# Two ScalarE copies moved up between a unit's products, and the last unit's sums and store rearranged

## The chip, the core and the metric

The kernel runs on one core of a Trainium2 chip. The metric is the device time of one execution in microseconds. The engines are TensorE (PE, with its weight loads as PEld), VectorE (DVE), ScalarE (ACT), GpSimd (POOL) and SyncE (SP), which only issues DMAs here.

## The reference

```python
a = softmax(phi, axis=2)                  # batch, n_heads, seq, n_mem = 8, 8, 576, 32
k_m, v_m = einsum('bhsm,bhsd->bhmd', a, k), einsum('bhsm,bhsd->bhmd', a, v)
attn = softmax(q @ k_m.T / sqrt(64))      # head_dim 64
x = (attn @ v_m) as (4608, 512)
h = x @ w_in                              # 512 x 2048
out = (h - tanh(h)) @ w_out               # 2048 x 512, f32
```

Tokens are pooled into 32 memory slots per head, attended to from every token, and put through a two-layer network whose middle function is h - tanh(h).

## The kernel before

Operands in f32 are split into a high and a low f16 part, and each product of TensorE is a sum of products of parts. The 4608 tokens are taken in 18 units of 256 (`UT`), and the 2048 middle columns in four blocks of 512 (`fb`), so there are 72 steps (u, fb). The attention of the eight batches, the conversion of the weights and checks of their range are spread over the steps by tables (`START`, `PLAN`, `PLAN3`, `PLAN_C`). The engines take their instructions in the order of the program text (`in_order`).

From unit 4 on, a step does the following. `mm1` computes the block's middle values into the PSUM tile `hs`. Then a chain of ScalarE and VectorE turns them into g = h - tanh(h) by a short polynomial: ScalarE squares `hs` into `u` (L579), VectorE multiplies (`g1`, L587), ScalarE squares again (`g1_square`, L592), VectorE multiplies (`g2`, L597), ScalarE rounds to f16 (`g2_high`, L603), and POOL forms the low part (`g3`, L608). VectorE also forms sums and differences of blocks of g, the tile `f` (`a_forms`, L621).

The second layer, `mm2_blocks`, runs two steps behind `mm1` and takes seven block products in place of eight (Winograd's form of Strassen's method on 2 x 2 blocks). m1, m5, m6 and m7 accumulate in the PSUM tile `x`, shape 128 x 2 x 512 f32: m1 in `x[:, 0, lo]`, m5 in `x[:, 0, hi]`, m6 in `x[:, 1, lo]`, m7 in `x[:, 1, hi]`, where `lo` and `hi` are the first and second 256 columns. m2, m3 and m4 go straight into the output accumulators `o[0]` and `o[1]`, as does `main`, the one product that the low parts don't double. Each of m1 to m7 is four matmuls (`prod`, L715), `main` is L708, and L702 in the last unit, where a part of `o[1]` goes to a PSUM tile of its own, `oh`. There is one tile `x` for the whole run.

After the fourth block of a unit (`last`) the four parts of `x` are combined. ScalarE copies m1 into `ra[:, 1]` (L753) and m5 into `rb[:, 2]` (L754), where `ra` and `rb` are SBUF tiles (`r` in the profile). Later in the step `evict` has VectorE add m6 and m7 to them (L768, L769), form two more sums (L770, L773), add `o[0]` and `o[1]` (L780, and L777 in the last unit) and store 128 rows at a time (L781 on SP; the last 128 rows at L778 on ScalarE's queue).

In the text of a step, `mm1` and the square at L579 come first, then L587, L592, `a_forms`, L597, then `mm2_blocks` with the two copies, then L603 and the rest. So the copies stand behind L592 on ScalarE. Waits between engines are worked out by the framework from the order of the text, tile by tile: an instruction that writes a tile waits for those ahead of it in the text that read it, and one that reads it waits for those ahead that wrote it.

Of the kernel before, what the change touches and what calls it, by code (L numbers as in the profile page):

```python
# [14 lines left out]
ALU = mybir.AluOpType  # L15
# [3 lines left out]
P = 128  # L19
# [4 lines left out]
NUNIT = B * S // UT  # L24
# [313 lines left out]
def split_path(ctx, tc, c, ins, out):  # L338
    nc = tc.nc
# [295 lines left out]
    acc = {}  # L635
# [50 lines left out]
    def mm2_blocks(u, fb, first, last):  # L686

        f, gg = gs.pop((u, fb))
        x = acc["x"]
        if first:
            acc[u] = [ps_o.tile([P, DM], F32, tag=f"o{i}", name=f"o{u}{fb}{i}") for i in range(2)]
        o = acc[u]
        ws = (wout_hi, wout_lo)

        def main(th):
            if th and u == NUNIT - 1:
                for dst, cs, end in ((acc["h1"], hi, last), (o[1][:, lo], lo, False)):  # L700
                    for k in range(4):
                        nc.tensor.matmul(  # L702
                            dst, gg[:, 0, k, P : 2 * P], wout_hi[:, 4 * fb + k, cs],
                            start=(first and k == 0), stop=(end and k == 3),
                        )
                return
            for k in range(4):
                nc.tensor.matmul(  # L708
                    o[th], gg[:, 0, k, P * th : P * th + P], wout_hi[:, 4 * fb + k, :], start=(first and k == 0), stop=False
                )  # L710

        def prod(dst, a, b, new=False, end=False):
            for kk in range(2):
                for n in range(2):
                    nc.tensor.matmul(  # L715
                        dst, a(1 - n, kk), b(n, kk), start=(new and kk == 0 and n == 0), stop=(end and kk == 1 and n == 1)
                    )

        def ab(th, kh):
            return lambda n, kk: gg[:, n, 2 * kh + kk, P * th : P * th + P]  # L720

        def af(i):
            return lambda n, kk: f[:, n, i, kk]

        def bb(kh, nh):
            return lambda n, kk: ws[n][:, 4 * fb + 2 * kh + kk, 256 * nh : 256 * nh + 256]

        def bf(i):
            return lambda n, kk: bts[i][:, n, fb, kk]

        lo, hi = slice(0, 256), slice(256, 512)
        if first and u == NUNIT - 1:
            acc["h1"] = ps_a.tile([P, 2, 512], F32, tag="pa", name="oh")[:, 0, lo]
        m1 = (x[:, 0, lo], ab(0, 0), bb(0, 0), first)
        m2 = (o[0][:, lo], ab(0, 1), bb(1, 0))
        m3 = (o[0][:, hi], af(0), bb(1, 1))
        m4 = (o[1][:, lo], ab(1, 1), bf(3))
        m5 = (x[:, 0, hi], af(2), bf(0))
        m6 = (x[:, 1, lo], af(3), bf(1), first)
        m7 = (x[:, 1, hi], af(1), bf(2))  # L740
        if not last:
            for m in (m1, m5, m6, m7) if first else ():
                prod(*m)
            main(0)
            main(1)
            for m in (m2, m4, m3) if first else (m2, m4, m1, m5, m6, m7, m3):
                prod(*m)
            return
        sc = 1.0 / (S_G * S_W)
        ra, rb = (big.tile([P, 3, 256], F32, tag="pr", name=f"r{u}{i}") for i in range(2))  # L750
        for m, end in ((m1, False), (m5, True), (m6, False), (m7, True)):
            prod(*m, end=end)
        nc.scalar.activation(ra[:, 1], x[:, 0, lo], AF.Copy, scale=sc)  # L753
        nc.scalar.activation(rb[:, 2], x[:, 0, hi], AF.Copy, scale=sc)  # L754
        for th, ms in ((0, (m2, m3)), (1, (m4,))):
            main(th)
            for m in ms:
                prod(*m, end=m is ms[-1])
        acc["evict"] = (u, ra, rb)

    def evict():
        if "evict" not in acc:
            return
        u, ra, rb = acc.pop("evict")
        x, o, t0 = acc["x"], acc[u], u * UT
        sc = 1.0 / (S_G * S_W)
        lo, hi = slice(0, 256), slice(256, 512)
        nc.vector.scalar_tensor_tensor(ra[:, 0], x[:, 1, lo], sc, ra[:, 1], op0=ALU.mult, op1=ALU.add)  # L768
        nc.vector.scalar_tensor_tensor(rb[:, 0], x[:, 1, hi], sc, ra[:, 0], op0=ALU.mult, op1=ALU.add)  # L769
        nc.vector.tensor_tensor(ra[:, 2], ra[:, 0], rb[:, 2], op=ALU.add)  # L770
        for th, r in ((0, ra[:, 1:3]), (1, rb[:, 0:2])):
            if th == (u == NUNIT - 1):
                nc.vector.tensor_tensor(rb[:, 1], rb[:, 0], rb[:, 2], op=ALU.add)  # L773
            r = r.rearrange("p a x -> p (a x)")
            if u == NUNIT - 1 and th == 1:
                for cs, p in ((hi, acc["h1"]), (lo, o[1][:, lo])):
                    nc.vector.scalar_tensor_tensor(r[:, cs], p, sc, r[:, cs], op0=ALU.mult, op1=ALU.add)  # L777
                nc.scalar.dma_start(out[t0 + P :, :], r)  # L778
                continue
            nc.vector.scalar_tensor_tensor(r, o[th], sc, r, op0=ALU.mult, op1=ALU.add)  # L780
            nc.sync.dma_start(out[t0 + P * th : t0 + P * th + P, :], r)  # L781
# [114 lines left out]
    for sl, (u, fb) in enumerate(slots, 18):  # L896
# [20 lines left out]
        queue.append((u, fb))  # L917
        v, vb = queue.pop(0)
        mm2_blocks(v, vb, vb == 0, vb == NFB - 1)
        while squared:  # L920
            window_sum(*squared.pop(0))
# [3 lines left out]
        while due and due[0][0] == "C":  # L925
            step(due.pop(0), True)
        evict()
        forms.append((u, fb))
        do(2)
# [3 lines left out]
    for u, fb in queue:  # L933
        mm2_blocks(u, fb, fb == 0, fb == NFB - 1)
    c["wide"] = nc.values_load(c["bad"][0:1, 0:1], min_val=0, max_val=1)
    evict()
    in_order(tc, c["first"])

# [215 lines left out]
```

## Time and profile before

| | |
|---|---|
| median of 3 runs | 659.96 us (659.03 to 661.41) |
| profiled execution, its own time | 659.43 us |
| its span, first to last instruction | 657.6 us |
| granted TensorE clock, mean | 0.995 |
| busy PE / DVE / ACT / POOL | 642.2 / 523.6 / 375.8 / 251.0 us |
| copies L753 and L754, 14 of each | 5.1 and 5.2 us busy |
| products into `x` (L715) | 896 matmuls |
| stores of `r`, 28, 256 KB each | 2.4 us from issue to landing (median) |

Times in rows are in microseconds from the span's start. "Idle before" and an arrow name the instruction that ended an engine's idle time. Matmuls overlap: a row's duration is from its start to its modelled end, while the next one starts earlier. The granted clock is the share of full speed that TensorE was given. The profiled execution's time is 1.83 us over its span, and 0.53 under the median.

### The profile page before, as it was taken

How to read it: one execution, taken by the hardware profiler on the slowest of the kernel's cores; microseconds unless marked ns; L12 is line 12 of the kernel's file. 1: busy time of each engine (PE TensorE's matmuls, PEld its weight loads, DVE VectorE, ACT ScalarE, POOL GpSimd, SP SyncE). 2: the span in 40 equal slices, each digit the busy share in tenths (PEclk: the TensorE clock that was granted, in tenths of full speed). 3: DMA queues.
4: the chain of work that ended last, by engine and by line, in shares of the span. 5: the costliest groups of instructions: out<-in, count | busy, mean ns of one | idle time of the engine just before them, and what ended most of it. 6: DMA issues, size and time to landing. Idle time of an engine off the chain costs nothing.

```text
span 657.6 us, 15599 instructions
## 1 busy us (share of the span) xinstructions
PE 642.2 (98%) x6690; PEld 456.3 (69%) x6690; DVE 523.6 (80%) x790; ACT 375.8 (57%) x509; POOL 251.0 (38%) x173
## 2 busy tenths in 40 slices
PE   8889999999999999999999999999999999999996
PEld 4355656566557777777776677877687777887885
DVE  6899999999855787875898679777978686867773
ACT  4577686666424456545655466545654677666541
POOL 0225141222222245451535353624452555455531
PEclk9899999999999999999999999999999999999999
DMA  9999345301423301324331515142415333234201
GB/s 343 377 365 393 109 170 180 117 3 65 146 97 102 138 28 74 113 91 145 105 113 66 168 51 168 37 162 70 146 41 197 98 101 117 63 117 136 86 33 37
DMA packets 25996, 84.98 MB, mean 129 GB/s; under 512 B 2880, under 2 KB 2880, under 8 KB 25152
## 3 DMA queue, kind: packets, MB, share of 16 engines
q1 hardware_dynamic: 24624, 81.55, 35.9%
q10 hardware_dynamic: 1296, 2.36, 0.9%
q8 instruction: 54, 0.88, 0.6%
q14 instruction: 22, 0.18, 0.1%
HBM read 72.37 MB, written 11.53 MB: 128 GB/s over the span
## 4 chain that ended last, share of the span: by engine, by line
PE 79%; DVE 11%; DMA 4%; ACT 2%; issue 2%; POOL 1%; SPq 0%; DVEq 0%; ACTq 0%; POOLq 0%
PE hs L572 20%; PE x L715 13%; PE o L708 13%; PE o L715 10%; PE o L651 6%; PE h L572 4%; PE o1h L651 3%; PE pp L524 3%; DMA raw<-in_w_out_dram 2%; PE pkv L220 2%; DMA kv<-in_kva_dram 2%; PE warm L789 1%; DVE wt L384 1%; DVE h L597 1%; DVE h L587 1%
## 5 line engine op out<-in xcount | busy, mean ns | idle before, releaser
L608 POOL TENSOR_TENSOR g<-h,g 128x1024 f16<-128x1024 f32 x64 | 138.5, 2165 | 327.3 <-ACT g L603 233.3
L572 PEld LDWEIGHTS <-ph 128*128 128x128 f16 x2304 | 176.9, 98 | 20.5 <-issue 6.0
L572 PE MATMUL hs<-ah,ph 128*128 128x256 f16 (+3 forms) x1152 | 151.5, 246 | 0.0
L587 DVE SCALAR_TENSOR_TENSOR h<-hs,u 128x1024 f32<-128x1024 f32 x54 | 65.8, 1219 | 91.0 <-ACT u L579 90.9
L603 ACT ACTIVATE g<-h 128x1024 f16<-128x1024 f32 x72 | 75.9, 1055 | 92.3 <-DVE h L597 90.2
L572 PE MATMUL hs<-al,ph 128*128 128x256 f16 (+3 forms) x576 | 127.6, 246 | 0.0
L592 ACT ACTIVATE u<-u,beta 128x1024 f32<-128x1024 f32 x72 | 82.4, 1147 | 55.5 <-DVE h L587 54.4
L708 PE MATMUL o<-wout_hi,g 128*128 128x512 f16 x432 | 104.7, 379 | 0.0
L715 PEld LDWEIGHTS <-f 128*128 128x128 f16 x896 | 87.7, 98 | 10.1
L597 DVE SCALAR_TENSOR_TENSOR h<-u,h 128x1024 f32<-128x1024 f32 x72 | 87.4, 1216 | 0.8 <-ACT u L592 0.7
L579 ACT ACTIVATE u<-hs 128x1024 f32<-128x1024 f32 x54 | 55.0, 1019 | 52.8 <-PE hs L572 48.3
L715 PEld LDWEIGHTS <-g 128*128 128x128 f16 x672 | 64.2, 98 | 26.5 <-issue 5.1
L715 PE MATMUL x<-bt,f 128*128 128x256 f16 x672 | 82.5, 273 | 0.0
L708 PEld LDWEIGHTS <-g 128*128 128x128 f16 x432 | 40.5, 98 | 43.9 <-issue 8.1
L621 DVE TENSOR_TENSOR f<-g 128x512 f16<-128x512 f16 x112 | 65.7, 626 | 4.3 <-POOL g L608 3.4
L651 PEld LDWEIGHTS <-g 128*128 128x128 f16 x384 | 36.7, 98 | 46.5 <-issue 3.4
L651 PE MATMUL o<-wout_hi,g 128*128 128x512 f16 x192 | 58.8, 379 | 0.0
L572 PE MATMUL h<-ah,ph 128*128 128x256 f16 (+3 forms) x384 | 49.6, 246 | 0.1
L572 PE MATMUL h<-al,ph 128*128 128x256 f16 (+2 forms) x192 | 42.4, 246 | 0.2 <-POOL al L515 0.2
L542 DVE SCALAR_TENSOR_TENSOR ph<-pp,ph 128x1024 f16<-128x1024 f32 x31 | 37.6, 1213 | 0.6 <-ACT ph L537 0.6
L537 ACT ACTIVATE ph<-pp 128x1024 f16<-128x1024 f32 x32 | 32.5, 1017 | 7.5 <-PE pp L524 7.4
L651 PE MATMUL o<-wout_lo,g 128*128 128x512 f16 x96 | 36.4, 379 | 0.0
(146 smaller groups left out, 980.0 us busy)
## 6 DMA issues: line engine op xcount, KB each, us to landing
kv<-in_kva_dram SPq DMA_DIRECT2D x20, 516.0 KB, 4.1
q<-in_qt_dram SPq DMA_DIRECT2D x16, 576.0 KB, 4.9
chk<-in_w_in_dram SPq DMA_DIRECT2D x16, 512.0 KB, 5.7
chk<-in_w_out_dram SPq DMA_DIRECT2D x16, 512.0 KB, 3.4
out_dram<-r SPq DMA_DIRECT2D x27, 256.0 KB, 2.4
kv<-in_kva_dram SPq DMA_DIRECT2D x6, 1032.0 KB, 8.8
raws<-in_w_in_dram SPq DMA_DIRECT2D x12, 512.0 KB, 7.1
raw<-in_w_out_dram SPq DMA_DIRECT2D x12, 512.0 KB, 7.2
```

Source lines behind the costliest of these rows:

```text
L542: nc.vector.scalar_tensor_tensor(pl, pa, S_P / (S_V * S_W), ph, op0=ALU.mult, op1=ALU.subtract)
L572: nc.tensor.matmul(hp[:, k, tu : tu + w], px[:, g, cs], d[ax][:, g, ta : ta + w], start=(n == 0), stop=(n == 5),)
L579: nc.scalar.activation(uu, hp, AF.Square, scale=1.0 / (S_A * S_P))
L587: nc.vector.scalar_tensor_tensor(h3, hp, C2 * S_G / (S_A * S_P), uu, op0=ALU.mult, op1=ALU.mult)
L592: nc.scalar.activation(uu, uu, AF.Square, bias=c["beta"])
L597: nc.vector.scalar_tensor_tensor(h3, uu, CC, hp, op0=ALU.add, op1=ALU.mult)
L603: nc.scalar.activation(gg[:, 0], h3, AF.Copy)
L608: eng.tensor_tensor(gg[:, 1], h3, gg[:, 0], op=ALU.subtract)
L621: nc.vector.tensor_tensor(o, x, y, op=op)
L651: nc.tensor.matmul(o, gx[:, k, P * tt : P * tt + P], wx[:, 4 * fb + k, :], start=(first and k == 0 and wx is wout_hi and gx is gh), stop=( ...
L708: nc.tensor.matmul(o[th], gg[:, 0, k, P * th : P * th + P], wout_hi[:, 4 * fb + k, :], start=(first and k == 0), stop=False)
L715: nc.tensor.matmul(dst, a(1 - n, kk), b(n, kk), start=(new and kk == 0 and n == 0), stop=(end and kk == 1 and n == 1))
```

## The change

In a unit's last block the two copies are issued behind m1 and m5 and ahead of m6 and m7. In `evict` the add L773 always stands ahead of the sums with `o`; in the last unit it stood between them. The last unit's second 128 rows are stored in two halves of 256 columns, each as soon as its sum is there, the first on SP and the second on ScalarE's queue.

```diff
-        for m, end in ((m1, False), (m5, True), (m6, False), (m7, True)):
+        for m, end in ((m1, False), (m5, True)):
             prod(*m, end=end)
         nc.scalar.activation(ra[:, 1], x[:, 0, lo], AF.Copy, scale=sc)
         nc.scalar.activation(rb[:, 2], x[:, 0, hi], AF.Copy, scale=sc)
+        for m, end in ((m6, False), (m7, True)):
+            prod(*m, end=end)
...
         nc.vector.tensor_tensor(ra[:, 2], ra[:, 0], rb[:, 2], op=ALU.add)
+        nc.vector.tensor_tensor(rb[:, 1], rb[:, 0], rb[:, 2], op=ALU.add)
         for th, r in ((0, ra[:, 1:3]), (1, rb[:, 0:2])):
-            if th == (u == NUNIT - 1):
-                nc.vector.tensor_tensor(rb[:, 1], rb[:, 0], rb[:, 2], op=ALU.add)
             r = r.rearrange("p a x -> p (a x)")
             if u == NUNIT - 1 and th == 1:
-                for cs, p in ((hi, acc["h1"]), (lo, o[1][:, lo])):
+                for cs, p, q in ((hi, acc["h1"], nc.sync), (lo, o[1][:, lo], nc.scalar)):
                     nc.vector.scalar_tensor_tensor(r[:, cs], p, sc, r[:, cs], op0=ALU.mult, op1=ALU.add)
-                nc.scalar.dma_start(out[t0 + P :, :], r)
+                    q.dma_start(out[t0 + P :, cs], r[:, cs])
                 continue
```

No engine's order changes in units 4 to 16; what changes is who waits. On TensorE, unit 4's last block, from m5's last product (`bt0`, weights from `f43`) to m6 (`bt1`); the names in brackets are the semaphores of the engines waited for:

```order
 L715 MATMUL x_2448<-bt0_1865,f43_2746 128x256
 L715 LDWEIGHTS f43_2746 [waits DVE_49]
-L715 MATMUL x_2448<-bt1_2110,f43_2746 128x256
+L715 MATMUL x_2448<-bt1_2110,f43_2746 128x256 [waits Activation_49]
 L715 LDWEIGHTS f43_2746
 L715 MATMUL x_2448<-bt1_2110,f43_2746 128x256
```

m6's first product has a wait for ScalarE that it had not; the count that it waits for is that of the second copy, L754. All fourteen units have it. A step later on TensorE, at m1 of unit 5 (`g50`), the first product that overwrites `x`:

```order
 L524 LDWEIGHTS vh3_2741
 L524 MATMUL pp30_2931<-win_lo_98,vh3_2741 32x512
-L715 LDWEIGHTS g50_2792 [waits DVE_49,Pool_49]
-L715 MATMUL x_2448<-wout_hi_99,g50_2792 128x256 [waits Activation_49]
+L715 LDWEIGHTS g50_2792 [waits Pool_49]
+L715 MATMUL x_2448<-wout_hi_99,g50_2792 128x256 [waits DVE_49]
 L715 LDWEIGHTS g50_2792
 L715 MATMUL x_2448<-wout_lo_100,g50_2792 128x256
```

The wait for the same count of ScalarE stood here, a step behind the copies, and is gone from here. On VectorE, the sums of the last unit (`r170` is `ra`, `r171` is `rb`, `o1700` and `o1701` are `o[0]` and `o[1]`), before:

```order
L768 SCALAR_TENSOR_TENSOR r170_8660<-x_2448,r170_8660 128x256 [waits DMAHW0_49,PE_49,Activation_49]
L769 SCALAR_TENSOR_TENSOR r171_8661<-x_2448,r170_8660 128x256 [waits DMAHW1_49,DVE_49]
L770 TENSOR_TENSOR r170_8660<-r170_8660,r171_8661 128x256
L780 SCALAR_TENSOR_TENSOR r170_8660<-o1700_8491,r170_8660 128x512 [waits DVE_49,PE_49]
L773 TENSOR_TENSOR r171_8661<-r171_8661 128x256
L777 SCALAR_TENSOR_TENSOR r171_8661<-oh_8493,r171_8661 128x256 [waits DVE_49,PE_49]
L777 SCALAR_TENSOR_TENSOR r171_8661<-o1701_8492,r171_8661 128x256 [waits PE_49]
```

and with the change:

```order
L770 SCALAR_TENSOR_TENSOR r170_8660<-x_2448,r170_8660 128x256 [waits DMAHW0_49,PE_49,Activation_49]
L771 SCALAR_TENSOR_TENSOR r171_8661<-x_2448,r170_8660 128x256 [waits DMAHW1_49,DVE_49]
L772 TENSOR_TENSOR r170_8660<-r170_8660,r171_8661 128x256
L773 TENSOR_TENSOR r171_8661<-r171_8661 128x256 [waits DVE_49]
L781 SCALAR_TENSOR_TENSOR r170_8660<-o1700_8491,r170_8660 128x512 [waits DVE_49,PE_49]
L778 SCALAR_TENSOR_TENSOR r171_8661<-oh_8493,r171_8661 128x256 [waits DVE_49,PE_49]
L778 SCALAR_TENSOR_TENSOR r171_8661<-o1701_8492,r171_8661 128x256 [waits PE_49]
```

The add L773 has moved ahead of the sum with `o[0]`; the two sums of the second half stand where they stood, and a store follows each.

## The prediction

> **What bounds the kernel now.** I read the page first, then the busy time of one long middle stretch, then the waits of TensorE.
>
> ```profile
> span 657.6 us, 15599 instructions
> PE 642.2 (98%) x6690; PEld 456.3 (69%) x6690; DVE 523.6 (80%) x790; ACT 375.8 (57%) x509; POOL 251.0 (38%) x173
> ```
>
> From 60 to 650 us (view by stretches; after the stretch and its length: PE, PEld, DVE, ACT and POOL busy, then the granted clock, DMA share and GB/s):
>
> ```profile
> 60.00:650.00 590.00, 588.31 (x6145) 425.96 (x6144) 470.43 (x696) 339.50 (x450) 238.01 (x155) 1.00 0.32 106
> ...
> PE pkv L220 <- DMA kv<-in_kva_dram: 1.3, 2, 1.0
> ```
>
> TensorE stands still for 1.69 of those 590 us. All that is added to TensorE's stream is added to the time, and at most 1.7 us of idle time can be taken back by a later wait that shrinks. So the question at every edit is what TensorE must wait for.
>
> **Where the moved copies stand.** The timeline of unit 4's last step, all engines; columns are start, duration, engine, line, operation:
>
> ```profile
> 222.09 1.02 ACT L579 ACTIVATE u<-hs 128x1024 f32<-128x1024 f32 x1 [2.56 <-PE hs L572]
> 222.32 1.47 PE L715 MATMUL x<-bt,f 128*128 128x256 f16 x12
> 223.14 1.22 DVE L587 SCALAR_TENSOR_TENSOR h<-hs,u 128x1024 f32<-128x1024 f32 x1 [2.93 <-ACT u L579]
> ...
> 224.40 1.15 ACT L592 ACTIVATE u<-u,beta 128x1024 f32<-128x1024 f32 x1 [1.29 <-DVE h L587]
> ...
> 225.46 0.37 ACT L753 ACTIVATE r<-x 128x256 f32<-128x256 f32 x1
> 225.72 0.37 ACT L754 ACTIVATE r<-x 128x256 f32<-128x256 f32 x1
> ...
> 226.23 0.60 PE L715 MATMUL o<-bt,g 128*128 128x256 f16 x4
> ...
> 228.34 1.28 DVE L780 SCALAR_TENSOR_TENSOR r<-o,r 128x512 f32<-128x512 f32 x2
> ...
> 229.55 1.02 ACT L579 ACTIVATE u<-hs 128x1024 f32<-128x1024 f32 x1 [1.43 <-PE hs L572]
> ```
>
> The row of twelve products holds m5 (four), m6 and m7. They start every (1.47 - 0.27) / 11 = 0.109 us, so m6 starts at 222.32 + 4 x 0.109 = 222.76. ScalarE gets to the copies only at 225.46, because they are queued behind a chain that begins when mm1 ends: square of hs, VectorE's L587, square L592, copies. They do not wait for the products at all; over the whole run they did once, in the last unit:
>
> ```profile
> its engine sat idle before it (us, times) until:
>   PE x L715: 5.2, 1
> ```
>
> So letting the copies wait for eight products in place of sixteen starts no copy earlier in units 4 to 16: the gain there is nil. But the order shows that m6's first product now waits for ScalarE; in the text it comes behind the copies, and it writes the tile x that they read. Before, this wait stood on the next unit's m1, where the copies were long done. The second copy ends at 226.09, 3.33 us after m6 started. Behind m6 on TensorE's queue stand m7, main and m2 to m4, then the next mm1, so TensorE stands still.
>
> **The stalls.** The same stretch, from m6's start to the second copy's end, for units 4 to 16 (columns as above; shortest, one of the middle, longest and the sum):
>
> ```profile
> 222.76:226.09 3.33, 3.33 (x26) 2.33 (x24) 2.91 (x6) 2.04 (x4) 0.00 (x0) 1.00 0.99 375
> ...
> 288.05:290.50 2.45, 2.45 (x21) 1.82 (x19) 2.28 (x6) 1.69 (x3) 0.83 (x1) 1.00 0.80 258
> ...
> 355.46:358.16 2.70, 2.70 (x23) 2.04 (x21) 2.57 (x3) 1.69 (x3) 2.18 (x2) 1.00 0.85 266
> ...
> 459.66:463.23 3.57, 3.57 (x27) 2.44 (x25) 3.44 (x5) 2.34 (x6) 3.48 (x4) 1.00 0.42 119
> ...
> 529.01:533.12 4.11, 4.11 (x38) 2.93 (x36) 2.95 (x3) 2.82 (x6) 3.97 (x4) 1.00 0.34 107
> 562.66:567.14 4.48, 4.48 (x48) 3.29 (x46) 2.92 (x5) 3.19 (x6) 3.16 (x3) 1.00 0.29 99
> ...
> sum 42.70, PE 42.70 PEld 30.42 DVE 37.25 ACT 27.65 POOL 32.09; mean PE 3.28 PEld 2.34 DVE 2.87 ACT 2.13 POOL 2.47
> ```
>
> Seven stalls lie at 3.33 to 3.57, four at 2.45 to 2.70, two above 4. TensorE is busy for all 42.70 us now and would be idle in them. The chain hangs on mm1's end, not on m6, so the stall does not shorten itself. I add 0.03 per unit from the end of a copy to the start of who waits, as in the last unit below: 13 x 0.03 = 0.4. **Stalls: 43.1 us.**
>
> VectorE is also queued behind this: its sum with o[1] (second of the two at 228.34) must wait for m4, which ends at 226.23 + 0.60 = 226.83 now and about 230.2 then. That work is done near 230.9, while the next square, now at 229.55, moves to 232.9: VectorE is free before its next L587. TensorE gets no second wait from it.
>
> **The clock.** A stall of 3 us may also slow the matmuls after it. The granted clock in this run falls twice, at 26.71 and at 654.76, 184 lengths of 3.413 us apart, so I cut the run on that grid (columns as above):
>
> ```profile
> 19.88:23.29 3.41, 2.25 (x52) 1.12 (x50) 2.72 (x7) 2.27 (x4) 1.23 (x2) 1.00 1.02 367
> 23.29:26.71 3.42, 1.58 (x26) 0.77 (x26) 2.99 (x6) 1.94 (x7) 1.04 (x1) 1.00 1.00 376
> 26.71:30.12 3.41, 3.41 (x37) 0.65 (x22) 3.07 (x5) 1.23 (x2) 0.88 (x1) 0.50 0.93 355
> ...
> 651.35:654.76 3.41, 0.98 (x10) 0.64 (x7) 1.77 (x4) 0.00 (x0) 0.00 (x0) 1.00 0.41 153
> 654.76:657.57 2.81, 0.00 (x0) 0.00 (x0) 0.00 (x0) 0.00 (x0) 0.00 (x0) 0.50 0.10 31
> ```
>
> A window in which TensorE was busy for 2.25 us kept the clock; after one with 1.58, and one with 0.98, the next ran at 0.50. What half costs, by warm-up products of one shape inside and behind the slow window:
>
> ```profile
> 27.18 1.03 PE L789 MATMUL warm<-nid 128*128 128x512 f16 x2
> ...
> 30.12 1.03 PE L789 MATMUL warm<-nid 128*128 128x512 f16 x4
> ```
>
> Two products take what four take after it: a slow window loses half of the 3.41 us, 1.71, less half of the idle time that reaches into it.
>
> A stall of s leaves s - 0.16 idle, since m5's last product ends 0.16 behind the next one's slot. Where the window border cuts it is chance. With the limit at 3.42 - 1.58 = 1.84 us idle and a stall of 3.35 (idle 3.19): the first part is over 1.84 in 40% of the positions (loses 1.37 on average, as 0.68 of the idle time reaches into the slow window); the second part in another 40%, or all lies in one window in 6% (1.71 each); in 14% both parts are short and nothing is lost: 1.33 on average. The short ones give 1.0, the long ones 1.55, the sum 7 x 1.35 + 4 x 1.0 + 2 x 1.55 = 16.6. With the limit at 3.41 - 2.25 = 1.16 idle, the same working gives 1.85, 1.64 and 1.97: 23.4. I take 20, between the two. If dense products count for more than the small ones of the start did, only the row at 651.35 is a safe limit (2.43 idle): 0.84, 0 and 1.14, so 9.
>
> The Trainium skill, "TensorE: Matmul & The Clock Gate", section "What's actually happening", has the clock halved after at least one wholly idle window of about 3.4 us; by that the clock term would be near 0.6. The rows at 23.29 and 651.35 speak against it, each halved after a window with work in it.
>
> **The last unit.** Here nothing else holds ScalarE:
>
> ```profile
> 647.82 1.47 PE L715 MATMUL x<-bt,f 128*128 128x256 f16 x12
> 649.33 0.38 ACT L753 ACTIVATE r<-x 128x256 f32<-128x256 f32 x1 [5.24 <-PE x L715]
> 649.61 0.38 ACT L754 ACTIVATE r<-x 128x256 f32<-128x256 f32 x1
> 650.02 0.42 DVE L768 SCALAR_TENSOR_TENSOR r<-x,r 128x256 f32<-128x256 f32 x1 [2.14 <-ACT r L754]
> ...
> 651.74 0.60 PE L715 MATMUL o<-bt,g 128*128 128x256 f16 x4
> ...
> 652.81 0.41 DVE L777 SCALAR_TENSOR_TENSOR r<-o,r 128x256 f32<-128x256 f32 x1
> 653.25 0.38 ACTq L778 DMA_DIRECT2D out_dram<-r  x1
> ...
> DMA to landing us min/median/max: 2.4/2.4/2.4
> ```
>
> m5 ends at 648.42, so the copies run from 648.46 to 649.12 (0.66 both) and m6 starts at 649.15 in place of 648.26: TensorE 0.89 later, its last product ends at 653.23. The last VectorE sum then starts at 653.26 in place of 652.81 and the store at 653.70: 0.45 later. VectorE's own chain moves only by m7's end, 650.02 to 650.23, and has room; the add that now stands ahead of the first half's sum (0.42) lies in the wait for o[0]. The other half of the store goes to SP behind one earlier store, off the path. The last transfer has half the bytes; a 256 KB store lands in 2.4 us, and half of one is not in the trace: between 0 and 0.5 less, I take 0.2, as most of a small store is latency. **End: +0.25** (-0.05 to +0.45).
>
> **Sum**, on the profiled execution (659.43 us, span 657.6, 0.5 under the median of the runs): 659.43 + 43.1 + 20 + 0.3 = 722.8 us.
>
> **Rivals.**
> - Only a nearly idle window slows the clock, as at 651.35: 659.43 + 43.1 + 9 + 0.3 = 712. For it: small-array products filled the window at 23.29, and they may count less. Against: so they did in the one at 19.88, which kept the clock.
> - Stalls without a slower clock, by the skill's whole window: in this mechanism only the stalls of 3.57, 4.11 and 4.48 can hold one: 703.4.
> - Not slower: m6's wait is met early. It would need the copies done by m6's start, over 2.45 us sooner than they are in every unit; that decides. Then the end gains: VectorE's first sum starts at m7's end, 649.3, and the last at 652.4 behind m4, 0.4 early, with 0.2 from the store: 658.8, no measurable change. The Trainium skill, "PSUM — Partial Sum Buffer", section "PSUM bank collisions raise a hardware error", asks for guards by bank and quadrant, not by address. Copies and m6 touch different halves of x, 512 f32 each, one bank each by that page; a wait by bank would leave m6 free, but the order shows the wait.
> - The slow clock lasts two windows per stall: 20 more, 743. Against: the clock was back after one at 30.12.
>
> **Chances.** The likeliest, slowed by nearly every stall: 0.65 (719 to 727). Slowed by some: 0.17 (708 to 716). Whole windows only: 0.10. Not slower: 0.03. Two windows: 0.05. From 708 to 728 leaves out 0.18. Two executions agree within some 2 us, 0.3%, which is what a measurement can tell here; all cases but one are slower by more: slower 0.97, same 0.02, faster 0.01.
>
> **What would show it.** On TensorE thirteen gaps of 2.3 to 4.4 us ahead of m6, put down to ACT's r at L754; copies that still start behind the square of u; the granted clock at 0.50 in ten to sixteen windows, each behind such a gap; TensorE idle some 43 us more in the middle stretch. Wrong would be: no such gaps, or gaps with the clock at full, or a VectorE or POOL wait that turns up on TensorE in the steps between.

## The result and the profile after

The changed kernel takes 720.26 us (median of 6 runs, 718.24 to 722.13) against 659.96: a ratio of 1.0912, interval 1.0888 to 1.0935, 60 us slower. The forecast was 722.8, range 708 to 728. The profiled execution took 718.24 us, with a span of 716.5. Its page, then the stretch from 60 us to shortly before the last unit's copies, then TensorE's waits (columns as ahead):

```profile
span 716.5 us, 15592 instructions
...
PE 660.4 (92%) x6690; PEld 462.5 (65%) x6690; DVE 530.0 (74%) x790; ACT 376.0 (52%) x509; POOL 250.4 (35%) x173
```

```profile
60.00:704.00 644.00, 604.10 (x6119) 429.56 (x6118) 476.44 (x694) 339.30 (x448) 237.44 (x155) 0.97 0.29 97
```

```profile
PE x L715 <- ACT r L754: 37.3, 13, 4.0
PE x L715 <- DVE f L621: 3.3, 1, 3.3
```

TensorE stands still for 39.9 us of that stretch, where before it was 1.7, and all but 0.1 of it lies ahead of m6. The two rows together are fourteen gaps, one a unit; one of them (3.3) is put down to a VectorE row that ended about then. The last unit's gap is 0.75, so the thirteen others are 37.3 + 3.3 - 0.75 = 39.85 us. Unit 4, the same rows as before the change:

```profile
222.33 1.02 ACT L579 ACTIVATE u<-hs 128x1024 f32<-128x1024 f32 x1 [2.56 <-PE hs L572]
...
222.56 0.60 PE L715 MATMUL x<-bt,f 128*128 128x256 f16 x4
223.38 1.22 DVE L587 SCALAR_TENSOR_TENSOR h<-hs,u 128x1024 f32<-128x1024 f32 x1 [2.93 <-ACT u L579]
...
224.64 1.15 ACT L592 ACTIVATE u<-u,beta 128x1024 f32<-128x1024 f32 x1 [1.29 <-DVE h L587]
...
225.70 0.37 ACT L753 ACTIVATE r<-x 128x256 f32<-128x256 f32 x1
225.96 0.38 ACT L754 ACTIVATE r<-x 128x256 f32<-128x256 f32 x1
...
226.39 1.86 PE L715 MATMUL x<-bt,f 128*128 128x256 f16 x8 [3.22 <-ACT r L754]
```

The row of twelve products has split into four (m5) and eight (m6, m7). The copies start where they did beside the chain (directly behind L592), and m6 starts 0.05 us behind the second. The eight then take 1.86 us in place of 1.03. The windows of the clock show why:

```profile
222.33:225.74 3.41, 0.83 (x8) 0.59 (x7) 2.32 (x5) 2.12 (x3) 0.00 (x0) 1.00 0.98 365
225.74:229.15 3.41, 2.76 (x11) 1.57 (x11) 2.24 (x5) 1.65 (x4) 0.72 (x1) 0.50 0.38 153
229.15:232.57 3.42, 3.42 (x27) 2.51 (x26) 3.36 (x6) 0.00 (x0) 1.41 (x1) 1.00 0.00 0
259.87:263.28 3.41, 1.13 (x16) 0.88 (x14) 2.00 (x2) 1.76 (x2) 3.41 (x3) 1.00 0.00 0
263.28:266.70 3.42, 2.41 (x10) 1.43 (x10) 2.96 (x6) 3.04 (x7) 0.03 (x1) 0.50 0.03 5
266.70:270.11 3.41, 3.41 (x13) 1.76 (x12) 3.41 (x4) 0.25 (x1) 2.36 (x1) 0.50 0.00 0
372.51:375.92 3.41, 1.52 (x28) 1.06 (x21) 2.42 (x3) 2.12 (x3) 3.25 (x2) 1.00 0.49 138
375.92:379.34 3.42, 2.95 (x22) 2.15 (x22) 3.35 (x8) 1.36 (x3) 0.00 (x0) 1.00 0.45 176
```

After 0.83 us of work the next window ran at half clock; after 1.52 it kept its speed. Ten of the thirteen stalls slowed the clock, two of them for two windows (263.28 is the first). In the twelve slow windows TensorE was busy for 37.2 us; taken as half of that, the loss is 18.6 us.

### The profile page after: what moved, and what is told of

Same layout as the page of the kernel before. It is cut to its first block, busy times and chain, and to the rows that moved or that the text cites. A ratio compares the mean times of both kernels' runs of the same rounds, so it can differ in the third digit from the quotient of the medians.

```text
span 716.5 us, 15592 instructions
## 1 busy us (share of the span) xinstructions
PE 660.4 (92%) x6690; PEld 462.5 (65%) x6690; DVE 530.0 (74%) x790; ACT 376.0 (52%) x509; POOL 250.4 (35%) x173
## 4 chain that ended last, share of the span: by engine, by line
PE 68%; DVE 18%; ACT 7%; issue 4%; DMA 3%; POOL 0%; SPq 0%; ACTq 0%; DVEq 0%; POOLq 0%
PE hs L572 16%; PE o L708 12%; PE x L715 11%; PE o L715 9%; PE o L651 5%; DVE h L587 5%; PE h L572 4%; ACT u L579 3%; DVE f L621 3%; PE o1h L651 3%; PE pp L524 2%; DVE h L597 2%; DMA raw<-in_w_out_dram 2%; PE warm L790 1%; DVE wt L384 1%
## 5 line engine op out<-in xcount | busy, mean ns | idle before, releaser
L715 PE MATMUL x<-bt,f 128*128 128x256 f16 x672 | 90.6, 284 | 40.6 <-ACT r L754 37.3
L715 PEld LDWEIGHTS <-f 128*128 128x128 f16 x896 | 90.7, 101 | 56.2 <-issue 43.0
L708 PE MATMUL o<-wout_hi,g 128*128 128x512 f16 x432 | 113.4, 403 | 0.0
L592 ACT ACTIVATE u<-u,beta 128x1024 f32<-128x1024 f32 x72 | 82.4, 1147 | 50.9 <-DVE h L587 49.8
L715 PEld LDWEIGHTS <-g 128*128 128x128 f16 x672 | 65.6, 100 | 29.7 <-issue 9.4
L708 PEld LDWEIGHTS <-g 128*128 128x128 f16 x432 | 42.9, 103 | 48.8 <-issue 14.5
L651 PEld LDWEIGHTS <-g 128*128 128x128 f16 x384 | 36.7, 98 | 46.5 <-issue 3.4
L621 DVE TENSOR_TENSOR f<-g 128x512 f16<-128x512 f16 x112 | 60.6, 581 | 3.8 <-POOL g L608 3.4
L651 PE MATMUL o<-wout_hi,g 128*128 128x512 f16 x192 | 58.8, 379 | 0.0
```

The costliest lines, as they stand in the source:

```text
L592: nc.scalar.activation(uu, uu, AF.Square, bias=c["beta"])
L621: nc.vector.tensor_tensor(o, x, y, op=op)
L651: nc.tensor.matmul(o, gx[:, k, P * tt : P * tt + P], wx[:, 4 * fb + k, :], start=(first and k == 0 and wx is wout_hi and gx is gh), stop=( ...
L708: nc.tensor.matmul(o[th], gg[:, 0, k, P * th : P * th + P], wout_hi[:, 4 * fb + k, :], start=(first and k == 0), stop=False)
L715: nc.tensor.matmul(dst, a(1 - n, kk), b(n, kk), start=(new and kk == 0 and n == 0), stop=(end and kk == 1 and n == 1))
```

## The experiments

Beside each is the median of before on the same chip in the same rounds (660.22 for the first four, 660.04 for the last four). The theory: m6 waits for the second copy only because m6 and the copies share the tile x; the copies end late because of their place on ScalarE; and the gaps halve the clock. The rival causes: the sums and stores of the last unit, a cost of the wait as such, and a slower clock that has nothing to do with the gaps.

### The copies alone

The first hunk of the change and nothing else.

> Only the copies are moved; sums and store as before. If m6's wait for the second copy is the cause: thirteen gaps of 2.1 to 4.0 us on TensorE ahead of m6, ten to thirteen half-clock windows, 717.5 to 721 us, about 1 us under the whole change, whose two half stores land later. If the sums and the store carry the loss: within 2 us of before.

721.16 us (717.87 to 723.41), ratio 1.0937 (1.0915 to 1.0960). The waits of TensorE are those of the whole change:

```profile
PE x L715 <- ACT r L754: 37.3, 13, 4.0
PE x L715 <- DVE f L621: 3.3, 1, 3.3
```

The moved copies carry the whole loss. The median lies 0.16 over the range given, and not 1 us under the whole change; runs of this kernel differ by 5.5 us, so a microsecond can't be told here.

### The sums and stores alone

The second hunk, with the copies where they were.

> Only the sums and the store of the last unit are changed; copies where they were. If m6's wait is the cause: no gap ahead of m6, no half clock after the start, 659.5 to 661.5 us; from the end of m5 in the last unit to the end of the span about 0.8 us more than before, since the half stores took 2.7 and 3.1 us to land in the changed kernel against 2.4 for the whole one. If the sums and the store carry the loss: about 720 us.

661.42 us, ratio 1.0023 (1.0012 to 1.0033). The last unit's stores, and the landing of the two halves:

```profile
652.50 0.34 SPq L780 DMA_DIRECT2D out_dram<-r  x1
...
652.88 0.52 SPq L777 DMA_DIRECT2D out_dram<-r  x1
653.12 0.38 ACTq L777 DMA_DIRECT2D out_dram<-r  x1
...
DMA to landing us min/median/max: 3.0/3.0/3.1
```

The last store starts sooner (4.45 us behind m5's end; 4.84 before), but a half of 128 KB lands 3.0 to 3.1 us after its issue where the whole 256 KB landed after 2.4, and the span ends 10.26 us behind m5, 1.1 later than before (9.15). The expectation was 0.8 later. So this hunk costs about 1 us, 2% of the loss.

### TensorE kept busy in the stall

The copies alone, with ten products more between m5 and m6:

```diff
         nc.scalar.activation(rb[:, 2], x[:, 0, hi], AF.Copy, scale=sc)
+        for _ in range(10 if u < NUNIT - 1 else 0):
+            nc.tensor.matmul(o[0], c["nid16"], c["zero16"].to_broadcast((P, DM)), start=False, stop=False)
         for m, end in ((m6, False), (m7, True)):
```

> Copies moved as in the change, sums and store as before; between m5 and m6 of units 4 to 16 ten products of 512 columns with a moving operand of zeros, added to o[0], which changes no number (10 x 0.216 = 2.16 us, less than the shortest stall). If the gaps halve the clock: m6 starts behind the second copy as late as with the change, the 41.9 us of stalls stay, no half-clock window in units 4 to 16, 699 to 704 us. If the slower clock has another cause, or costs nothing on the path: 717 to 721 us. If the added products lengthen the path themselves: 13 x 2.16 = 28 us more, near 747 us.

699.48 us (699.08 to 699.77), ratio 1.0596 (1.0578 to 1.0613). Clock, and unit 4 again:

```profile
core 0: 698.0 us, clock 0.999
```

```profile
223.52 2.34 PE L756 MATMUL o<-zero,nid 128*128 128x512 f16 x10
...
226.48 0.37 ACT L754 ACTIVATE r<-x 128x256 f32<-128x256 f32 x1
...
226.91 1.03 PE L715 MATMUL x<-bt,f 128*128 128x256 f16 x8 [1.05 <-ACT r L754]
```

m6 still starts only behind the second copy, but no window of units 4 to 16 is slow, and the eight products take 1.03 us again. 130 extra products make the kernel 21.7 us faster than the copies alone (721.16 - 699.48): that is the clock's part. Its runs lie within 0.7 us. The four of the copies alone lie within 5.5, and as their time rises from 717.87 to 723.41 us their granted clock falls from 0.968 to 0.961. Which stalls slow the clock differs from one execution to the next: the stalls of units 6 and 8 slowed it in the profile of the copies alone and not in that of the whole change, the stall of unit 9 the other way round.

### The copies ahead of the square on ScalarE

The copies alone, with the second layer's step of a unit's last block ahead of the square at L592:

```diff
+        queue.append((u, fb))
+        v, vb = queue.pop(0)
+        if vb == NFB - 1:
+            mm2_blocks(v, vb, vb == 0, True)
         g1_square(u, fb)
         a_forms(*forms.pop())
         g2(u, fb)
-        queue.append((u, fb))
-        v, vb = queue.pop(0)
-        mm2_blocks(v, vb, vb == 0, vb == NFB - 1)
+        if vb < NFB - 1:
+            mm2_blocks(v, vb, vb == 0, False)
```

> Copies moved as in the change, sums and store as before; in a unit's last block the second layer's step is issued ahead of the square at L592, so that on ScalarE the copies stand ahead of it, in its idle time, and no longer behind it. TensorE's order and its wait are those of the change. If the stall is the copies' place on ScalarE's queue: stalls of 0.9 to 1.1 us (two near 2), in sum some 15 us, no half clock, 672 to 679 us. If the wait itself or the copies' own 0.66 us made the stall: near 720 us.

671.80 us (670.95 to 672.13), ratio 1.0175 (1.0157 to 1.0192), 0.2 under the range given. The timeline of unit 4 and the waits of TensorE:

```profile
222.94 1.02 ACT L579 ACTIVATE u<-hs 128x1024 f32<-128x1024 f32 x1 [2.56 <-PE hs L572]
...
223.85 0.38 ACT L753 ACTIVATE r<-x 128x256 f32<-128x256 f32 x1
...
224.12 0.39 ACT L754 ACTIVATE r<-x 128x256 f32<-128x256 f32 x1
224.56 1.03 PE L715 MATMUL x<-bt,f 128*128 128x256 f16 x8 [0.79 <-ACT r L754]
```

```profile
PE x L715 <- ACT r L754: 12.8, 14, 1.6
```

The same wait, with nothing but the copies' place on ScalarE changed: gaps of 12.8 us in all in place of 40.6, and no slow window. Stalls of up to 1.6 us pay their own length and no clock.

### The unit's other products between m5 and m6

The copies alone, with `main`, m2, m3 and m4 of units 4 to 16 issued ahead of m6 and m7.

> Copies moved as in the change, sums and store as before; in units 4 to 16 main, m2, m3 and m4 stand between m5 and m6 on TensorE, 3.04 us of the unit's own work, and m6 waits for the second copy as in the change. If the stall is only TensorE's lack of other work: gaps ahead of m6 of 0.2 to 1.1 us, some 4.5 us in sum and none in the four units with short stalls, no half clock in units 4 to 16, with the 0.6 us at the end 663 to 667 us. If a wait of TensorE for ScalarE costs by itself: 13 x 1 us or more, from 673 us on.

666.46 us (665.13 to 667.39), ratio 1.0093 (1.0064 to 1.0122).

```profile
PE x L715 <- ACT r L760: 4.2, 10, 0.9
PE pkv L220 <- DMA kv<-in_kva_dram: 1.8, 2, 1.4
PE hs L572 <- POOL al L515: 0.9, 1, 0.9
```

The wait stands in the program as with the change and costs 4.2 us, 0.75 of them in the last unit, where TensorE has its own work to do meanwhile. In the four units whose stalls were short it costs nothing. A wait is no cost as such.

### Two tiles for x, with the whole change and with the copies alone

```diff
-            acc["x"] = ps_h.tile([P, 2, 512], F32, tag="h", name="x")
-            acc["hp"] = ps_h.tile([P, 4, UT], F32, tag="h", name="hs")
+            until_18.close()
+            ps_x = ctx.enter_context(tc.tile_pool(name="ps_x", bufs=1, space=PSUM))
+            acc["x"] = [ps_x.tile([P, 512], F32, tag=f"x{i}", name=f"x{i}") for i in range(2)]
+            acc["hp"] = ps_x.tile([P, 4, UT], F32, tag="h", name="hs")
```

Here `until_18` holds the pool `ps_h`, and `x[:, i, ...]` becomes `x[i][:, ...]`.

> The whole change, but x is two tiles of one bank each (m1 and m5 in the one, m6 and m7 in the other), so m6 writes a tile that no copy reads. If the wait comes from the one tile: no wait for ScalarE ahead of m6, no gap, no half clock, 660 to 662 us, over before only by the stores in halves. If ScalarE's reading beside TensorE's writing, or the copies' place, costs by itself: above 663 us.

> Copies moved and x as two tiles, sums and store as before. If the theory holds: no gap in units 4 to 16; in the last unit VectorE's first sum starts 0.6 us sooner after m5's end than before, and the span's end comes 0.3 to 0.5 us sooner after m5's end: 659.4 to 660.4 us, no change that can be told from before by the time.

With the whole change 660.22 us, ratio 1.0000 (0.9986 to 1.0014); with the copies alone 659.32, ratio 0.9991 (0.9974 to 1.0009), 0.08 under the range given. Neither can be told from before by the time. The 60 us are gone with the shared tile. All waits of TensorE from 60 us on, with the whole change and two tiles:

```profile
PE pp L525 <- ACT wn L484: 0.3, 1, 0.3
PE pkv L220 <- DMA kv<-in_kva_dram: 0.2, 1, 0.2
```

Unit 4 of the same run; the numbers of lines are one higher here:

```profile
222.41 1.47 PE L716 MATMUL x<-bt,f 128*128 128x256 f16 x12
...
225.54 0.36 ACT L754 ACTIVATE r<-x 128x256 f32<-128x256 f32 x1
225.81 0.38 ACT L755 ACTIVATE r<-x 128x256 f32<-128x256 f32 x1
```

m5, m6 and m7 are one row of twelve again, and the copies come 3 us behind it. In the last unit, with the copies alone:

```profile
648.48 0.38 ACT L754 ACTIVATE r<-x 128x256 f32<-128x256 f32 x1 [4.37 <-PE x L716]
648.76 0.38 ACT L755 ACTIVATE r<-x 128x256 f32<-128x256 f32 x1
...
649.41 0.42 DVE L771 SCALAR_TENSOR_TENSOR r<-x,r 128x256 f32<-128x256 f32 x1 [1.51 <-PE x L716]
...
653.01 0.38 ACTq L781 DMA_DIRECT2D out_dram<-r  x1
```

m5's end is at 648.44, so the first sum starts 0.97 us behind it (1.60 before), the last store 4.56 (4.84 before), and the span ends 8.90 behind (9.15 before). A quarter of a microsecond is what the earlier copies are worth in this profile, a little less than the 0.3 to 0.5 expected. It is below what the times can tell.

### Both halves on ScalarE's queue

The sums and stores alone, with the first half on ScalarE's queue too.

> The changed sums of the last unit with both half stores on ScalarE's queue; copies where they were. Theory from the end of the trace: the span ends some 3.1 us behind the landing of SP's last store or some 1.9 us behind that of ScalarE's, whichever is later, because SP goes through a row of waits behind its store; with no half on SP its last landing is the earlier store's, and the end comes back to 9.1 to 9.4 us behind m5's end (9.15 before, 10.26 with a half on SP): 659.7 to 660.7 us. If halves as such land late: it stays near 10.2 us behind m5, 661.4 us.

660.22 us, ratio 1.0002 (0.9990 to 1.0015).

```profile
652.86 0.34 SPq L780 DMA_DIRECT2D out_dram<-r  x1
...
653.15 0.89 ACTq L777 DMA_DIRECT2D out_dram<-r  x2
...
DMA to landing us min/median/max: 2.9/3.0/3.1
```

The span ends 9.13 us behind m5, as before the change. The halves take as long to land as on two queues. The last one is issued 0.24 us sooner behind m5 than the whole store was before and lands 0.27 later, and the end stays where it was; so the late landing alone is not the cost. The extra 1.1 us comes with the half on SP. SP's last store lands 6.31 us behind m5 here and 7.19 with the half on SP, and in all the profiles of this case the span ends 2.4 to 3.2 us behind that landing. That SP goes through its closing waits one after the other would explain it; it was not tried by itself.

## Why the prediction was right, point by point

- **TensorE sets the time, and 1.7 us at most come back.** The first half held: outside the gaps its idle time in the middle stretch fell from 1.7 to under 0.1 us. But some 3 us came back (see the sum).
- **The stalls, 43.1 us.** Right in mechanism and size: 39.85 us of gaps and 13 x 0.16 us from m5's drain make 41.9. Counted so, the four short ones came out at 2.3 to 2.5 in place of 2.45 to 2.70, and the longest at 4.0 in place of 4.48. `copies_only` shows that the hunk carries it, `early` that the length is the queue on ScalarE, the two tiles that the wait is that of the shared tile.
- **No second wait on TensorE.** Held with the change; with the other products ahead of m6 one of 0.9 us turned up.
- **The clock, 20 us.** Right in kind and size: 18.6 in the profiled execution by half the busy time, 18.1 by the comparison under the sum, 21.7 from the medians with and without filled stalls. The limit under it was off. I put it between 1.16 and 1.84 us idle from products of the start; for these dense ones it lies near 2: a window with 1.42 us of work slowed the next, one with 1.44 did not.

```profile
372.94:376.35 3.41, 1.42 (x24) 0.97 (x17) 2.50 (x2) 2.12 (x4) 3.21 (x2) 1.00 0.50 156
376.35:379.77 3.42, 3.05 (x12) 1.69 (x12) 3.35 (x8) 1.35 (x3) 0.00 (x0) 0.50 0.40 158
...
413.90:417.31 3.41, 1.44 (x11) 1.07 (x11) 3.38 (x6) 3.09 (x7) 2.07 (x2) 1.00 0.75 211
```

  (This is the run with the copies alone.) So the rival "small products count less" was right in its direction, though not with its limit of 2.43: a window with 1.58 us of the products of the start slowed the next, one with 1.44 of the dense ones did not. By the prediction's working that takes some microseconds off; two slow phases of two windows each, which the prediction gave 0.05 as the rule for every stall, gave about as much back. That the size came out so close is in part luck. (The rival's own price was added up wrongly: 7 x 0.84 + 2 x 1.14 is 8.2, not 9.) The rule of an idle window (the Trainium skill, "TensorE: Matmul & The Clock Gate", section "What's actually happening"), read as a window without any work, is not borne out here: windows with 0.83, 1.13 and 1.42 us of work slowed the next.
- **The end, +0.25 us.** This step failed in size: from m5's end to the span's end it took 10.66 us in place of 9.15, 1.5 more. The last unit's m5, the last store and the landing of the two halves:

```profile
705.19 0.60 PE L715 MATMUL x<-bt,f 128*128 128x256 f16 x4
...
711.11 0.38 ACTq L779 DMA_DIRECT2D out_dram<-r  x1
...
DMA to landing us min/median/max: 2.7/2.9/3.1
```

  The store started 0.48 later, as worked out (0.45). The term that was mis-sized is the last store, taken to land 0.2 sooner, bounded at 0 to 0.5: ScalarE's half took 2.7 us where 2.4 was shown, 0.3 more, and another 0.8 came between its landing and the end (2.65 in place of 1.89), which `halves_scalar` puts down to the half on SP.
- **The sum.** By spans 716.5 - 657.6 = 58.9. Unit 4's m5 starts 0.24 us later than before. From m5 to m6 the thirteen units take 41.96 longer in all, from m6 to the next unit's m5 15.17 longer, and the end 1.5: together 58.9. With the stalls filled, where the clock stayed at full, the way from m6 to the next m5 is 2.97 shorter than before. So the slow windows took 18.1 of this execution, and 3.0 came back, of which 1.6 are waits that show as idle time of TensorE before; what the rest was is not shown. The forecast for a profiled execution was 43.1 + 20 + 0.3 = 63.4 more, which is 4.5 too much. The median lies closer to the forecast because the profiled execution was the fastest of the six.

## What to carry to other kernels

A copy out of an accumulator that is moved ahead of products into the same tile puts a wait into TensorE's stream, even if they write other columns; look where the reader really stands on its own queue, since that, not its dependence, sets how long TensorE waits. Price such a gap twice: by its length, and by the clock. Here gaps of up to 1.6 us cost no clock, and of thirteen gaps of 2.15 to 4.0 us ten cost one or two windows of 3.41 us at half speed. Give parts with different readers tiles of their own, or put the engine's other work between.

## What the runs showed of the hardware that was not expected

A busy window doesn't always give a slow clock back: after a slow window with 2.41 us of work (the row at 263.28) the next was slow too, after one with 2.76 (225.74) it was not, though at full clock 1.52 was enough to keep it. Part of this may be that a product takes nearly twice as long at half clock (1.86 us for eight in place of 1.03), so 2.41 us there are, by an estimate from these rows, the work of 1.2 to 1.3 at full clock. Whether busy time or work counts, these rows don't settle.

VectorE's sums between SBUF tiles (L772, L773 after the change), always 0.41 to 0.42 us before, took up to 1.98 and 2.35 when the stall moved them behind the start of a subtraction on POOL; each then ended 0.3 us after an instruction of POOL. Sums that start ahead of the subtraction keep their 0.42 though they run into it: before, L773 did so in all thirteen units, 0.12 to 0.19 us ahead. It lies off the path:

```profile
228.43 2.12 POOL L608 TENSOR_TENSOR g<-h,g 128x1024 f16<-128x1024 f32 x1 [6.47 <-ACT g L603]
...
229.14 1.70 DVE L772 TENSOR_TENSOR r<-r,r 128x256 f32<-128x256 f32 x1
```

Halves of a store mostly took longer to land than the whole: 2.7 to 3.1 us against 2.4 on one queue as on two, in the split kernel 2.2 on ScalarE's queue and 3.6 on SP. With the halves on two queues the issue on SP took 0.52, 0.94 and 1.35 us in place of 0.34.
